# A linear-attention and gated FFN block on one NeuronCore: tokens as columns in the down and last attention products, two products summed in PSUM, another count of transfers, another order

## The chip, the core and the metric

The kernel runs on one core of a Trainium2 chip. The core has TensorE (PE) for matrix products, VectorE (DVE), ScalarE (ACT) and GpSimd (POOL) for elementwise work, and SyncE (SP), which issues the transfers between DRAM and the on-chip memory (SBUF). Products land in PSUM, which has 8 banks of 128 x 512 fp32. The metric is the device time of one execution in microseconds (us), as the median over runs.

## What is computed

x has 2048 tokens of width D = 512. A layer norm feeds two branches: linear attention with 32 heads of width 16, and a gated FFN of width F = 1792. The output is x plus the product of the two.

```python
phi = lambda t: jnp.where(t > 0, t + 1, jnp.exp(t)) + 1e-6
q, k, v = heads(xn @ wqkv)                      # xn = layernorm(x)
pq, pk = phi(q), phi(k)
kv = jnp.einsum("bhsd,bhse->bhde", pk, v)
z = jnp.einsum("bhsd->bhd", pk)
num = jnp.einsum("bhqd,bhde->bhqe", pq, kv)
den = jnp.einsum("bhqd,bhd->bhq", pq, z)[..., None] + 1e-6
s = (num / den) @ wo
g = silu((gelu(xn @ w_gate) * (xn @ w_up)) @ w_down)
return x + s * g
```

## The kernel before

**Precision.** Every large product is made in the fp32r format from operands split in two parts, hi and lo. `split` (L469) makes hi by a cast on ACT and lo = source − hi on DVE. `three` (L500) pairs them as hi·hi, hi·lo and lo·hi, so each product takes three matmuls per block of 128 in the summed dimension, and `Sum` (L475) issues them as separate steps into one PSUM bank.

**Strassen.** The large products use the seven-product Strassen-Winograd form, with the operand forms of `PRODUCTS` (L63). The seven products are summed into four results named 11, 12, 21 and 22; result 11 is product 1 plus product 2.

**First stage** (`first_products` L759, `rest` L787). Tokens are taken in eight pairs of 128-row tiles. Layer norm, transposes on PE, operand forms on POOL and splits give the matrices Xh and Xl. Pairs 0 and 1 make k and q plainly; pairs 2 to 7 make them by seven products, keys ("A", n, i). In `first_products` ACT saves product 1 (`e1`), PE makes product 2 in bank Y, and DVE adds the two. `gacc` (L747) sums the matrix from which kv follows, keys ("G", t, c), and POOL sums phi(k) into `zacc`. The X matrices of the first four pairs are written to DRAM (`spill_x`, L754) and read back for the second pass.

**FFN** (`ffn` L1127), in two passes over 1024 tokens: p = 1 has the second half of the tokens, p = 0 the first. Each pass has 7 units u of 256 gate and 256 up columns. A `quad` (L1037) makes the gate (even q) or the up part (odd q) of a unit by seven products ("F", q, i) of six 512-column matmuls: banks X = 0 or 1, Y = 2, Z = 3 or 4. Product 1 is saved by ACT (`fe`), product 2 goes to bank Y, and DVE adds. For the gate, ACT then takes gelu; for the up part, POOL multiplies by the gate. Result 21 has no add: ACT or DVE reads it from PSUM. Units 0 to 4 are multiplied with w_down by seven products ("E", p, u, v, i) in `down_strassen` (L1000), where h is the stationary operand and the down weights, 256 columns wide, are the moving one. Each bank of 512 columns takes two such regions r. DVE adds each bank to the sums `acc` (in the first unit ACT copies), whose tiles are 128 tokens by 512 features. Units 5 and 6 are multiplied plainly in `down` (L1095), keys ("D", p, u, j, c). The last of the eight tiles is made in two halves (`halves`, L1091).

**Attention** (`attn` L1229), between the passes. The matrix M (kv times wo) is made and split. `attn` then takes the 16 token tiles one by one, in the `order` 8, 0, 9, 1 and so on: a load of q, a product with z on POOL, the denominator and its reciprocal on DVE, the normalised tile pn, four transposes ("QT", i), a split, and twelve matmuls ("S", i) with pq stationary and M moving. Tiles 8 to 15 are multiplied by the finished g, x is added, and the result is stored; tiles 0 to 7 are stored as `s_d` and read back in `finish0` (L1288). z itself (`run_z`, L1196) is a product of ones with `zacc`, made amid the plain down products of pass 1, with the result in `zb`.

**Order.** Nothing runs in the order of the text. Each `do` (L121) records an operation with its engine and an estimated cost. `Plan.order` (L160) then simulates the engines (`forward`, L289) and picks, on each engine, the ready operation with the earliest due time. PE follows the list `pe_keys`, with a view of 6 us ahead (`AHEAD`). The draws of `KEPT` (L19) repeat fixed random changes of due times (`altered`, L183). The order that comes out is fixed in the program; on the chip each engine works through its own list and waits by semaphores. Transfers go through one list on SP; `forward` counts them by their size in KB and the constants `RATES` and `HELD`.

## Time and profile before

| | |
|---|---|
| median of 3 runs | 618.93 us (618.93 to 620.43) |
| profiled execution, its own time | 620.97 us |
| its span, first to last instruction | 619.3 us |
| granted TensorE clock, mean | 0.999 |
| DRAM traffic | 67.63 MB read, 44.56 MB written, 181 GB/s over the span |

The stages, as busy us of each engine in each stretch:

| stretch | us | PE | DVE | ACT | POOL |
|---|---|---|---|---|---|
| first stage, 8.68 to 136 | 127.32 | 125.07 | 107.36 | 96.03 | 64.96 |
| gate and up with down, pass 1, 136 to 328.7 | 192.70 | 192.65 | 163.24 | 107.67 | 92.85 |
| plain down and M, 328.7 to 357.3 | 28.60 | 28.60 | 22.83 | 11.50 | 10.70 |
| attention, 357.3 to 407.85 | 50.55 | 50.55 | 41.42 | 13.01 | 13.69 |
| pass 0, 407.85 to 613 | 205.15 | 205.15 | 139.25 | 89.48 | 47.23 |

In a row of groups, `L494 PE MATMUL FX<-Xh,w 128*128 128x512` names line, engine, operation, the tile written and those read, and the shape; after it come the count, the busy time and the mean ns of one. Line 494 is that of `Sum`'s matmul, so products are told apart by their tiles: FX, FY, FZ are gate and up, dX, dY, dZ the seven down products, d the plain ones, X, Y, Z the first stage, sps the attention's last product. A matmul's duration reaches from its start to its modelled end and overlaps the next; PEld is the load of the stationary operand. A row of waits has the engine, its line and tile, whom it waited for, and then the total in us, the number and the longest.

### The profile page before, as it was taken

The numbers are of one execution on the slowest core, as the hardware profiler recorded it, in microseconds if no ns is written. First come the engines' busy times: TensorE is split into PE (matmuls) and PEld (weight loads), VectorE is DVE, ScalarE is ACT, GpSimd is POOL, SyncE is SP. The second block draws the span as 40 slices with busy tenths as digits, with TensorE's granted clock in tenths as the row PEclk, the third lists the DMA queues.
The fourth block names the chain that finished last, engine by engine and source line by source line (L and its number), as shares of the span: only waits on it lengthen the run. The fifth ranks groups of instructions, "written<-read, shape, count | busy, mean of one in ns | idle before, by whom it ended". The sixth has DMA issues, their size and how long they took to land.

```text
span 619.3 us, 8717 instructions
## 1 busy us (share of the span) xinstructions
PE 611.5 (99%) x3156; PEld 517.6 (84%) x3156; DVE 481.3 (78%) x785; ACT 323.1 (52%) x582; POOL 233.8 (38%) x223
## 2 busy tenths in 40 slices
PE   9998999999999999999999999999999999999997
PEld 8886788878888888898888788888888888988886
DVE  6998797687788998999957799634567778786656
ACT  6676777685676464556444323244554334343433
POOL 4446743366635456452414344023031314111110
PEclk9999999999999999999999999999999999999999
DMA  7158740157726264435579755864433334343255
GB/s 263 61 160 269 227 144 36 54 199 263 300 69 271 73 268 154 186 135 206 225 246 399 303 171 186 321 222 177 178 131 145 139 133 153 120 152 120 69 166 191
DMA packets 49083, 112.77 MB, mean 182 GB/s; under 512 B 3088, under 2 KB 24848, under 8 KB 45456
## 3 DMA queue, kind: packets, MB, share of 16 engines
q1 hardware_dynamic: 49040, 112.21, 50.6%
q8 instruction: 25, 0.41, 0.3%
q14 instruction: 18, 0.15, 0.1%
HBM read 67.63 MB, written 44.56 MB: 181 GB/s over the span
## 4 chain that ended last, share of the span: by engine, by line
PE 95%; DVE 2%; DMA 2%; ACT 1%; issue 1%; SPq 0%; DVEq 0%; ACTq 0%
PE FX L494 25%; PE FZ L494 12%; PE dX L494 9%; PE sps L494 7%; PE d L494 7%; PE gps L494 6%; PE FY L494 6%; PE dZ L494 5%; PE X L494 5%; PE dY L494 2%; PE Z L494 2%; PE k L494 2%; PE q L494 2%; DMA x<-in_A_x 2%; PE Y L494 1%; PE ptq L1248 1%
## 5 line engine op out<-in xcount | busy, mean ns | idle before, releaser
L1062 POOL TENSOR_TENSOR h<-h,g 128x512 f32<-128x512 f32 x42 | 60.6, 1442 | 208.1 <-DVE h L467 199.9
L494 PE MATMUL FX<-Xh,w 128*128 128x512 f32 x448 | 134.6, 393 | 0.0
L494 PEld LDWEIGHTS FX<-Xh,w 128*128 128x128 f32 x448 | 80.0, 188 | 15.0 <-ACT fu L461 1.2
L494 PE MATMUL FX<-Xl,w 128*128 128x512 f32 x224 | 69.1, 393 | 0.0
L494 PE MATMUL FZ<-Xh,w 128*128 128x512 f32 x224 | 68.2, 391 | 0.0
L461 ACT COPY fu<-FX 128x512 f32<-128x512 f32 x56 | 32.7, 584 | 50.3 <-PE FX L494 48.6
L1021 DVE TENSOR_TENSOR acc<-acc,dX 128x512 f32<-128x512 f32 x64 | 43.7, 682 | 14.5 <-PE dX L494 13.7
L494 PEld LDWEIGHTS FZ<-Xh,w 128*128 128x128 f32 x224 | 40.5, 188 | 7.2
L494 PEld LDWEIGHTS FX<-Xl,w 128*128 128x128 f32 x224 | 40.0, 188 | 7.7 <-ACT fu L461 1.0
L467 POOL TENSOR_TENSOR u<-q,mstuff 128x512 f32<-128x512 f32 x16 | 22.8, 1438 | 33.2 <-DMA q<-q_d 24.5
L981 ACT ACTIVATE g<-g 128x512 f32<-128x512 f32 x42 | 26.6, 633 | 16.6 <-DVE g L467 14.2
L467 DVE TENSOR_TENSOR h<-fu,FZ 128x512 f32<-128x512 f32 x28 | 19.2, 684 | 20.4 <-ACT fu L461 17.3
L737 POOL TENSOR_TENSOR zacc<-zacc,kp 128x512 f32<-128x512 f32 x16 | 22.7, 1416 | 32.6 <-DVE kp L726 31.7
L461 ACT CAST hfh<-sums 128x512 fp32r<-128x512 f32 x40 | 24.4, 622 | 20.1 <-DVE sums L467 20.0
L494 PE MATMUL FY<-Xh,w 128*128 128x512 f32 x112 | 34.7, 393 | 0.0
L494 PE MATMUL FZ<-Xl,w 128*128 128x512 f32 x112 | 34.7, 391 | 0.0
L467 POOL TENSOR_TENSOR tmp<-raw 128x256 f32<-128x256 f32 x28 | 26.7, 967 | 20.9 <-DVE w L467 11.8
L1021 DVE TENSOR_TENSOR acc<-acc,dZ 128x512 f32<-128x512 f32 x40 | 27.3, 682 | 8.1 <-PE dZ L494 7.4
L494 PE MATMUL dX<-dh,hfl 128*128 128x256 f32 x160 | 32.2, 283 | 0.0
L494 PE MATMUL dX<-dl,hfh 128*128 128x256 f32 x160 | 32.2, 282 | 0.0
L467 DVE TENSOR_TENSOR g<-fu,FZ 128x512 f32<-128x512 f32 x28 | 19.1, 683 | 16.4 <-PE FZ L494 9.1
L494 PE MATMUL dX<-dh,hfh 128*128 128x256 f32 x160 | 31.9, 281 | 0.0
(196 smaller groups left out, 1580.2 us busy)
## 6 DMA issues: line engine op xcount, KB each, us to landing
w_d<-w SPq DMA_DIRECT2D x14, 1792.0 KB, 9.2
w<-w_d SPq DMA_DIRECT2D x14, 1792.0 KB, 7.3
draw<-in_B_w_down SPq DMA_DIRECT2D x14, 512.0 KB, 3.7
x<-in_A_x SPq DMA_DIRECT2D x16, 256.0 KB, 4.6
q_d<-qp SPq DMA_DIRECT2D x16, 256.0 KB, 2.0
q<-q_d SPq DMA_DIRECT2D x16, 256.0 KB, 3.3
xh_d<-Xh SPq DMA_DIRECT2D x4, 896.0 KB, 4.9
xl_d<-Xl SPq DMA_DIRECT2D x4, 896.0 KB, 6.3
```

What stands on the lines that cost most here:

```text
L461: do("ACT", act(n), lambda o, i: nc.scalar.copy(o, i), dst, src, name=name)
L467: do(eng, c, lambda o, p, q: getattr(e, f"tensor_{op}")(o, p, q), dst, a, b, name=name)
L494: nc.tensor.matmul(o if r is None else o[:, r], a, b, start=first, stop=made == self.passes[r], skip_group_check=self.on or r is not None)
L737: do("POOL", pool(D), lambda o, i: nc.gpsimd.tensor_add(o, o, i), zacc, p0, name="zacc")
L981: do("ACT", act(NC), lambda o, i: nc.scalar.activation(o, i, AF.Gelu_apprx_tanh), v, src, name="gelu")
L1021: do("DVE", dve(D), lambda o, i: nc.vector.tensor_add(o, o, i), o, ps, name="acc")
L1062: do("POOL", pool(NC), lambda o, i: nc.gpsimd.tensor_mul(o, o, i), h, g, name="h")
L1248: nc.tensor.transpose(o[:, k, :], a[:, k * P:(k + 1) * P], b)
```

## The change

It has five parts.

1. The seven down products take the down weights as the stationary operand and h, 512 tokens wide, as the moving one. The plain down products and the last product of the attention swap their operands in the same way. `acc`, `s_d` and the output hold features in rows and tokens in columns; the host passes x a second time, transposed, and transposes the output. `attn` works on four chunks of 512 tokens, each of which transposes four normalised tiles and makes four ("S", i, n).
2. In the first stage, in gate and up, and in the down products, ACT copies product 1 from its bank into bank Y (`seed`), and PE sums product 2 on top. The add of the two falls away; gelu or the product with the gate reads Y.
3. z is made amid quad 0 of pass 1, after its products 1, 2, 6, 5 and 7; its result goes back into `zacc`, and `zb` falls away.
4. The planner counts transfers otherwise: other KB for strided or spilled ones, other constants, and a hold of SP behind writes named `spill`. ACT's estimate tells PSUM from SBUF.
5. Other orders in `pe_keys` and a shorter `KEPT`; three plain down keys of unit 5 move into the last quad of pass 0.

```diff
 EPS = 1e-6
 KEPT = [
-    (-1, 12, [5000002, 5000009, 5000018, 5000019, 5000024, 5000044, 5000060]),
...
-        5000002, 5000007, 5000009, 5000014, 5000018, 5000022, 5000026, 5000031, 5000033, 5000034,
...
+    (-1, 12, [9100221, 9100222]),
+    (55, 70, [9100172]),
 ]
...
-RATES = 260.0, 380.0
-
-HELD = 1.9
+RATES = 260.0, 385.0
+HELD = 1.3, 2.6
+BEHIND = 2.8
 
...
-                dma = max(dma, o.end) + o.kb * (1.4 if o.kb == 896 else 1.0) / (RATES[0] if o.end < 3.0 else RATES[1])
-                o.lat = max(dma - o.end, o.kb / self.RATE) + (1.1 if o.end < 8.0 else HELD)
+                if written > o.end:
+                    o.end = free["SP"] = max(o.end, dma - BEHIND)
+                dma = max(dma, o.end) + o.kb / (RATES[0] if o.end < 3.0 else RATES[1])
+                if o.name == "spill":
+                    written = dma
+                o.lat = dma - o.end + HELD[o.end > 10.0]
...
-def act(n):
-    return 0.065 + 0.00084 * n
+def act(n, psum=False):
+    return 0.06 + (0.00083 if psum else 0.00095) * n
...
-    s_d = dram_view([S // 2, D], "s_d", NT // 2)
+    s_d = dram_view([D, S // 2], "s_d", NT // 2)
...
     def spill_x(n):
         for hl in "hl":
             dma(x_d[hl](n, (slice(None), slice(None), slice(n * P, (n + 1) * P))),
-                xrows(hl, 0, 7, [n]).map(lambda ap: ap.bitcast(F32)), 896)
+                xrows(hl, 0, 7, [n]).map(lambda ap: ap.bitcast(F32)), 1390, "spill")
 
     def first_products(n):
         ta = tokens[n][0]
         X = bank(0, f"X{n}")
         prod(X, n, 1, True)
-        e1 = saved(X, f"e1_{n}")
         split_xn(ta)
         Y = bank(2, f"Y{n}")
-        prod(Y, n, 2, True)
-        k_out(added(e1, Y, f"c11_{n}"), ta)
+        copy("ACT", Y, X, D, "seed")
+        prod(Y, n, 2, False)
+        k_out(Y, ta)
         return X
 
...
         pe_keys.append(("A", n, 4))
         g_take(2)
         pe_keys.append(("A", n, 3))
-        g_take(2)
         if more:
             pe_keys.append(("A", n + 1, 1))
+        g_take(2)
...
+    ones_r = const("ones_r", [P, P], F32R)
+    copy("ACT", ones_r, ones, P)
+    zh, zl = tile_in("up", 34, [P, D], F32R, "zh"), tile_in("up", 35, [P, D], F32R, "zl")
+    split(zh, zl, zacc, D, "z")
+    pz = bank(7, "pz")
+
...
+    copy("ACT", zacc, pz, D, "zb")
+    zb3 = zacc.map(lambda ap: ap.rearrange("p (h d) -> p h d", d=DH))
+    do("DVE", 0.59, lambda o, i: nc.vector.tensor_reduce(o, i, axis=AX.X, op=ALU.add), den_eps, zb3, port=False)
...
-        dma(raw, ext((up_k if i else gate_k)[:, :, u * 2 * P:(u + 1) * 2 * P]), 512)
+        dma(raw, ext((up_k if i else gate_k)[:, :, u * 2 * P:(u + 1) * 2 * P]), 900)
...
-            dma(w.map(lambda ap: ap.rearrange("p a s c -> p (a s c)").bitcast(F32)), w_d(q - NQ, q - NQ), 1792)
+            dma(w.map(lambda ap: ap.rearrange("p a s c -> p (a s c)").bitcast(F32)), w_d(q - NQ, q - NQ), 2220)
...
-        dma(w_d(q, q), w.map(lambda ap: ap.rearrange("p a s c -> p (a s c)").bitcast(F32)), 1792)
+        dma(w_d(q, q), w.map(lambda ap: ap.rearrange("p a s c -> p (a s c)").bitcast(F32)), 2220, "spill")
...
-        dma(raw, ext(down_f[:, 2 * u:2 * u + 2, :]), 512)
+        dma(raw, ext(down_f[:, 2 * u:2 * u + 2, :]), 620)
...
     def down_strassen(p, u, first):
 
-        for v in range(2):
-            X, Y, Z = (bank(5 + i, f"d{c}{p}{u}_{v}", (P, 2, 2 * P)) for i, c in enumerate("XYZ"))
+        for r in range(2):
+            X, Y, Z = (bank(i, f"d{c}{p}{u}_{r}") for i, c in zip((7, 6, 5) if r else (5, 6, 7), "XYZ"))
 
             def prod(ps, i, on):
                 a, b = PRODUCTS[i]
-                ws_, xs_ = three([[f[:, (2 * v + r) * P:(2 * v + r + 1) * P] for f in hforms[u, b]] for r in range(2)],
-                                 [ds[u, a]] * 2), None
-                Sum(ps, on).add(("E", p, u, v, i), *[[(*ab, r) for r, ab in enumerate(part)] for part in ws_],
-                                name="down", cost=SHORT)
+                Sum(ps, on).add(("E", p, u, r, i), *three([[f[:, r * P:(r + 1) * P] for f in ds[u, a]]], [hforms[u, b]]), name="down")
 
             def out(ps, key, new=False):
 
                 half, chunk = {11: (0, 0), 21: (1, 0), 12: (0, 1), 22: (1, 1)}[key]
-                pair = accp[p, 2 * chunk + v]
-                o = pair.part([pair.res[2 * r + half] for r in range(2)],
-                              (slice(None), slice(None), slice(half * 2 * P, (half + 1) * 2 * P)))
+                o = acc[p, 4 * chunk + 2 * half + r]
                 if first and new:
                     copy("ACT", o, ps, D, "acc")
                 else:
                     do("DVE", dve(D), lambda o, i: nc.vector.tensor_add(o, o, i), o, ps, name="acc")
             prod(X, 1, False)
-            out(X, 11, True)
-            prod(Y, 2, False)
-            out(Y, 11)
+            copy("ACT", Y, X, D, "seed")
+            prod(Y, 2, True)
+            out(Y, 11, True)
             prod(X, 6, True)
             out(X, 12, True)
             prod(Z, 5, False)
+            out(Z, 22, True)
             prod(X, 7, True)
-            out(X, 22, True)
-            out(Z, 22)
+            out(X, 22)
+            prod(Z, 3, True)
+            out(Z, 12)
             prod(X, 4, True)
             out(X, 21, True)
-            prod(Z, 3, True)
-            out(Z, 12)
...
     def quad(q, p):
         u, is_up = divmod(q % NQ, 2)
...
         X, Y, Z = bank(q % 2, f"FX{q}"), bank(2, f"FY{q}"), bank(3 + q % 2, f"FZ{q}")
         fprod(X, q, 1, True)
-        e1 = esaved(X, f"fe1_{q}")
-        fprod(Y, q, 2, True)
-        c_out(11, e1, Y)
+        copy("ACT", Y, X, NC, "seed")
+        fprod(Y, q, 2, False)
+        c_out(11, None, Y)
...
                 for u in units_:
-                    hh, hl = hs[p, u, key[0]], hs[p, u, key[1]]
-                    dh, dl = dws[p, u]
-                    total.add(("D", p, u, j, c), *three([(h[0][:, sl], h[1][:, sl]) for h in (hh, hl)],
-                                                       [(dh[i][:, cs], dl[i][:, cs]) for i in range(2)]),
+                    total.add(("D", p, u, j, c), *three([[f[i][:, sl] for f in dws[p, u]] for i in range(2)],
+                                                       [[f[:, cs] for f in hs[p, u, k]] for k in key]),
                               name="down", cost=PASS if m == 1 else SHORT)
...
+        early = [("D", p, SD[p], j, 0) for j in range(0 if p else 3)]
         for q in range(base, base + NQ):
...
-            for n, pair in enumerate(((q, 6), (q, 5), (q, 7), (q + 1, 1), (q + 1, 2), (q, 4), (q, 3))):
+            for n, pair in enumerate(((q, 6), (q, 5), (q, 7), (q + 1, 1), (q, 4), (q + 1, 2), (q, 3))):
                 if pair[0] < base + NQ:
                     keys.append(("F", *pair))
                 if i == 0 and n == 3 and 0 < u <= SD[p]:
-                    wait += [("E", p, u - 1, v, m) for v in range(2) for m in (1, 2, 6, 5, 7, 4, 3)]
+                    wait += [("E", p, u - 1, r, m) for r in range(2) for m in (1, 6, 5, 2, 7, 3, 4)]
                 for _ in range(min(2 if i else 1, len(wait))):
                     keys.append(wait.pop(0))
+                if early and q == base + NQ - 1 and pair[1] in (7, 4, 3):
+                    keys.append(early.pop(0))
         keys += wait
-        return keys, lambda j: [("D", p, u, j, c) for c in range(halves(p, j)) for u in plain_units]
+        return keys, lambda j: [key for c in range(halves(p, j)) for u in plain_units
+                                for key in [("D", p, u, j, c)] if key not in keys]
...
     pe_keys += keys1[:2]
     g_take(100)
-    pe_keys += keys1[2:]
+    pe_keys += keys1[2:5] + ["z"] + keys1[5:]
...
-    zh, zl = U("fx", FX, "zh", F32R), U("fx", FX, "zl", F32R)
-    split(zh, zl, zacc, D, "z")
-    pz = bank(2, "pz")
...
-    order = [t for a, b in zip(range(8, 16), range(8)) for t in (a, b)]
+    CHUNKS = [2, 0, 3, 1]
...
     def attn(i):
+        c = CHUNKS[i]
+        pns = []
+        for t in range(4 * c, 4 * c + 4):
...
+        forms_ = []
+        for k in range(KT):
+            pt = bank(ring("spt", [0, 1]), f"ptq{c}{k}", (P, 4, P))
+
+            def run_t(o, b, *a, k=k):
+                for j in range(4):
+                    nc.tensor.transpose(o[:, j, :], a[j][:, k * P:(k + 1) * P], b)
+            do("PE", 0.45, run_t, pt, ident, *pns, key=("QT", i, k))
+            ptf = pt.map(lambda ap: ap.rearrange("p j c -> p (j c)"))
+            f = [tile_in("up", places[i % 2][k][hl], [P, NC], F32R, f"pqT{hl}{c}{k}") for hl in range(2)]
+            split(*f, ptf, NC, "pqT")
+            forms_.append(f)
+        for n in range(KT):
+            ps = bank(ring("sps", [3, 4, 2]), f"sps{c}{n}")
+            Sum(ps).add(("S", i, n), *three([[M[hl].part(M[hl].res[k:k + 1], (slice(None), k, slice(n * P, (n + 1) * P))) for hl in range(2)]
+                                             for k in range(KT)], forms_), name="S")
+            at = slice(n * P, (n + 1) * P), slice(c * NC, (c + 1) * NC)
+            if c >= 2:
+                g = acc[1, 4 * (c - 2) + n]
+                xr = U("sxr", FACC, f"sxr{c}{n}")
+                dma(xr, ext(xT[at]), 256)
+                do("DVE", dve(D), lambda o, i: nc.vector.tensor_mul(o, o, i), g, ps)
+                tt("DVE", "add", g, g, xr, D)
+                dma(ext(outT[at]), g, 256)
+            else:
+                so = U("sxr", FACC, f"so{c}{n}")
+                copy("ACT", so, ps, D, "so")
+                dma(s_d(4 * c + n, at), so, 256)
+
+    held = [hs[1, u, key][hl].unit for key in (11, 21, 12, 22) for u in range(SD[1], NU) for hl in range(2)]
+    spots = [s for s in [*FHH, *FHL] if s not in held] + held
+    places = [[spots[2 * k:2 * k + 2] for k in range(b, b + KT)] for b in (0, KT)]
+    for i in range(4):
         attn(i)
-    pe_keys += last1(0) + last1(1) + ["z"] + last1(2) + last1(3) + last1(4)
+    pe_keys += last1(0) + last1(1) + last1(2) + last1(3) + last1(4)
     pe_keys += [("kv", g) for g in range(KT)] + last1(5) + [("m", g) for g in range(KT)]
-    pe_keys += last1(6) + [("QT", 0)] + last1(7)
-    for i in range(NT):
-        if i + 1 < NT:
-            pe_keys.append(("QT", i + 1))
+    pe_keys += last1(6) + [("QT", 0, 0), ("QT", 0, 1)] + last1(7) + [("QT", 0, 2), ("QT", 0, 3)]
+    for i in range(4):
+        for n in range(KT):
+            pe_keys.append(("S", i, n))
+            if i < 3 and n < 3:
+                pe_keys += [("QT", i + 1, n)] + [("QT", i + 1, 3)] * (n == 2)
...
-        n = halves(p, j)
-        sr = U("fs", [*FG, *FX], f"fs{j}", parts=n)
...
-        dma(sr, s_d(j, slice(j * P, (j + 1) * P)), 256)
-        dma(xr, ext(x[j * P:(j + 1) * P, :]), 256)
+        rows, c = slice((j % 4) * P, (j % 4 + 1) * P), j // 4
+        at = rows, slice(c * NC, (c + 1) * NC)
+        dma(sr, s_d(j, at), 256)
+        dma(xr, ext(xT[at]), 256)
+        w = NC // m
...
+    laid = {name: _np.ascontiguousarray(inputs[name]) for name in _INS}
+    laid["A_x"] = laid["A_x"].reshape(shape[-2], shape[-1])
+    laid["A_xT"] = _np.ascontiguousarray(laid["A_x"].T)
...
+    return _np.ascontiguousarray(r.results[0]["out_yT"].T).reshape(shape)
```

151 lines of the change are left out of this document (56 added, 95 removed), and 7 rows, old and new, of the table KEPT.

## The prediction

> **What bounds the kernel now.** I began with the page, its shares and its 40 slices.
>
> ```profile
> span 619.3 us, 8717 instructions
> ...
> PE 611.5 (99%) x3156; PEld 517.6 (84%) x3156; DVE 481.3 (78%) x785; ACT 323.1 (52%) x582; POOL 233.8 (38%) x223
> ...
> PE   9998999999999999999999999999999999999997
> PEld 8886788878888888898888788888888888988886
> DVE  6998797687788998999957799634567778786656
> ```
>
> PE is busy in every slice except the one near 54 us and the two ends; the next engine, DVE, has 78%. The profiled execution took 620.97 us for a span of 619.3, so 1.7 us lie around the span; the three runs have the median 618.93, 2.04 below this execution. I make the sum against 620.97 and take 2.04 off.
>
> Next I asked what PE waited for between the first real product (8.6 us) and the last (613 us).
>
> ```profile
> PE X L494 <- DVE qp L726: 2.0, 1, 2.0
> PE Z L494 <- DVE c L467: 0.3, 1, 0.3
> ```
>
> That is the whole list: 2.3 us. So the time is the sum of the matmuls in PE's order, a head and a tail. An edit counts if it makes PE's stream shorter, takes away these 2.3 us, or puts a wait into the stream. Relief for DVE, ACT and POOL counts only through waits.
>
> A matmul's own duration (393 ns for 512 columns) overlaps its successor's; what counts is the pitch. I took it from the chain of waits, in a stretch that has only 512-column matmuls:
>
> ```profile
> 422.99 2.72 PE FX L494 x12
> 425.71 1.36 PE FY L494 x6
> ```
>
> 2.72/12 = 0.2267 us each. Then I read the two stretches that hold the down products of each pass, from the first to the last 256-column matmul, and the groups by shape for their number:
>
> ```profile
> 169.53:309.80 140.27, 140.27 (x813) 123.31 (x812) 128.65 (x204) 77.97 (x144) 66.90 (x62) 1.00 0.46 176
> 435.07:575.49 140.42, 140.42 (x813) 123.15 (x812) 104.64 (x162) 59.21 (x106) 31.60 (x26) 1.00 0.38 139
> ```
>
> ```profile
> L494 PE MATMUL dX<-dh,hfl 128*128 128x256 f32 x160 | 32.2, 283 | 0.0
> ...
> L494 PE MATMUL dZ<-dh,hfl 128*128 128x256 f32 x80 | 16.0, 281 | 0.0
> ...
> L494 PE MATMUL dY<-dh,hfl 128*128 128x256 f32 x40 | 8.0, 281 | 0.0
> ```
>
> The window's columns are length, PE, PEld, DVE, ACT and POOL busy with counts, clock, DMA share and GB/s. Each of the three kinds (hi·hi, hi·lo, lo·hi) has 160 + 80 + 40 = 280 matmuls of 256 columns, so there are 840, or 420 in each stretch. One of the 813 began before its window, which leaves 392 of 512 columns. At 0.2267 those take 88.9 us, and the other 51.4 us fall on 420 narrow ones: 0.1225 each. PE is full in both stretches, and in the first DVE is at 92%.
>
> **Down products with tokens as columns.** For each of 7 products, 2 halves, 10 units and 3 kinds, two 256-column matmuls become one of 512: 840 go, 420 come. At 0.2267 the two stretches become 2 × 812 less 420, that is 1204 × 0.2267 = 272.9 us against 280.7: 7.8 us less. That is one end. For the other I looked at narrow matmuls in a row:
>
> ```profile
> 300.23 0.40 PE L494 MATMUL dX<-dl,hfh 128*128 128x256 f32 x2
> 300.46 0.40 PE L494 MATMUL dX<-dh,hfl 128*128 128x256 f32 x2
> 300.70 0.63 PE L494 MATMUL FX<-Xl,w 128*128 128x512 f32 x2
> ```
>
> Four of them start within 300.23 to 300.70, 0.47 us, or 0.235 a pair: only 0.008 above one wide matmul, times 420 = 3.5 us. The rest of the 7.8 sits in the 512-column matmuls of the stretch, of which six in a row take more than 1.36:
>
> ```profile
> 287.74 1.39 PE FY L494 x6
> 289.84 1.39 PE FX L494 x6
> ```
>
> Whether these return to 1.36 depends on whether mixing widths slows them. In the pure stretch around 425 us not one six is slow, so I take 7.2, near the upper end, and keep 3.5 to 7.8.
>
> The Trainium skill (TensorE: Matmul & The Clock Gate, Back-to-back issue gap) says a warm matmul follows the last after its columns divided by 2.4 plus 2.5 ns, which makes 215.8 ns for 512 columns and 109.2 for 256. By that rule a pair is only 2.5 ns dearer than one, and this edit would save an estimated 1.1 us. By that rule the trace disagrees: it has 226.7 ns and 117 to 122 ns.
>
> The stationary side changes from h to the down weights, with half as many loads (PEld has 88% of the stretch, beside PE): nothing. The plain down products and the attention's last product keep their number and width: nothing.
>
> **Two products summed in PSUM.** In 54 places (6 in the first stage, 28 in gate and up, 20 in down) product 2 now starts on a copy of product 1 that ACT writes into its bank.
>
> ```profile
> L461 ACT COPY fe<-FX 128x512 f32<-128x512 f32 x28 | 16.4, 585 | 6.5 <-PE FX L494 6.4
> ...
> L461 ACT COPY e<-X 128x512 f32<-128x512 f32 x6 | 3.5, 585 | 3.4 <-PE X L494 3.4
> ...
> L461 ACT COPY d<-acc 128x512 f32<-128x512 f32 x1 | 0.6, 591 | 0.7 <-DVE acc L1118 0.7
> ```
>
> ```profile
> L1021 DVE TENSOR_TENSOR acc<-acc,dY 128x512 f32<-128x512 f32 x20 | 13.6, 678 | 2.4 <-PE dY L494 2.2 <-issue 0.2
> ...
> L467 DVE TENSOR_TENSOR g<-fe,FY 128x512 f32<-128x512 f32 x14 | 9.5, 682 | 7.0 <-PE FY L494 6.3 <-ACT fe L461 0.6
> ...
> L467 DVE TENSOR_TENSOR h<-fe,FY 128x512 f32<-128x512 f32 x14 | 9.5, 679 | 2.7 <-PE FY L494 2.7
> ...
> L467 DVE TENSOR_TENSOR c<-e,Y 128x512 f32<-128x512 f32 x6 | 4.1, 679 | 0.6 <-PE Y L494 0.6
> ```
>
> ```profile
> L1062 POOL TENSOR_TENSOR h<-h,g 128x512 f32<-128x512 f32 x42 | 60.6, 1442 | 208.1 <-DVE h L467 199.9 <-ACT fu L461 6.1 <-ACT hh L461 2.0
> ```
>
> 34 ACT copies only change their target. No copy from PSUM to PSUM is in the trace; the copy out of PSUM takes 585 ns and the one into it 591, so I take 0.59 and would allow 0.5 to 0.7. ACT gains 20 × 0.59 = 11.8 us. DVE loses 20 + 14 + 6 adds, 13.6 + 9.5 + 4.1 = 27.2 us; where product 11 of the up half was added (14 times) DVE now multiplies by the gate, and POOL loses 14 × 1.44 = 20.2 us. On PE's account all of it is zero, because PE is at 100% beside it.
>
> New is the wait: product 2 needs product 1, the copy, and then PE again. Its length, from rows:
>
> ```profile
> 415.12 1.08 PE L494 MATMUL FX<-Xh,w 128*128 128x512 f32 x4
> ...
> 416.29 0.59 ACT L461 COPY fe<-FX 128x512 f32<-128x512 f32 x1
> ```
>
> ```profile
> 57.47 0.65 DVE L726 SCALAR_TENSOR_TENSOR qp<-X,qr 128x512 f32<-128x512 f32 x1
> 58.18 1.19 PE L494 MATMUL X<-kq,Xh 128*128 128x512 f32 x4 [1.97 <-DVE qp L726]
> ```
>
> The product ends at 416.20 and ACT starts 0.09 later. A PE that waits for DVE starts about 0.06 after it; I use that for ACT. Chain: 0.09 + 0.59 + 0.06 = 0.74, plus 0.17 by which a matmul's end (0.393) lags its pitch: 0.91 us of PE if nothing stood between. The new order puts one product of six (1.36) between, product 4 of the quad before, and in units 1 to 5 two to four down products more; in the first stage two G keys of three matmuls, 1.36 again; in the down products 6 and 5 stand between 1 and 2, and 6, which must not touch X before the copy has read it, has a gate or up product ahead of it. So the cover is 0.45 us where it is thinnest, in units 0 and 6. There ACT may be in the middle of another operation (0.6), and late by at most 0.2. What queues behind such a wait on PE is the rest of its order; behind the copy on ACT, the next h and g conversions. Range 0 to 54 × 0.91 = 49; I take +0.2.
>
> **Attention in four chunks of 512 tokens.** PE's work is unchanged: 64 transposes and 192 matmuls.
>
> ```profile
> 357.53 2.76 PE sps L494 x12
> 360.73 2.77 PE sps L494 x12
> ```
>
> ```profile
> L461 ACT CAST pqTh<-ptq 128x512 fp32r<-128x512 f32 x16 | 9.4, 587 | 15.0 <-PE ptq L1248 15.0
> ```
>
> ```profile
> L467 DVE TENSOR_TENSOR pqTl<-ptq,pqTh 128x512 fp32r<-128x512 f32 x16 | 10.8, 678 | 4.1 <-ACT pqTh L461 4.1
> ```
>
> ```profile
> 357.30:407.85 50.55, 50.55 (x252) 41.76 (x250) 41.42 (x78) 13.01 (x24) 13.69 (x9) 1.00 0.61 210
> ```
>
> One S key with its four transposes takes 3.20 us, as it will. What changes is the grouping: the first transpose of a chunk needs all four normalised tiles, and its first S key all four splits. DVE is 82% busy here and keeps the same number of operations, so over 12.8 us (four keys) it has 2.3 to spare. The last split of the next chunk takes about 0.6 + 0.7 plus hops, 1.5 us, behind the S key placed after it (2.76): covered. The first chunk has only its own beginning: transposes 2 and 3 stand directly before S, at most two casts and a sub, 2 × 0.59 + 0.68 = 1.9 us, if PE's order takes nothing else in between. Bounds 0 to 1.9, and 7.6 if every chunk does it; I take +0.4. The loads of x and the stores of s and y keep their number and size (256 KB in rows of 2 KB) and pass SP's queue in another order; nothing on PE waits for them but the buffers of S.
>
> **z moved forward.** The two pz matmuls go from the plain down products to the first quad, with two casts, a sub, a copy and a reduce.
>
> ```profile
> L737 POOL TENSOR_TENSOR zacc<-zacc,kp x16: 1287/1298/1839, 15.1 to 139.0; 128x512 f32<-128x512 f32 x16
> ```
>
> POOL's last sum starts at 139.0 and ends near 141; the z key stands behind 8 G keys (24 matmuls, 5.4 us of PE) and three products (4.1) that begin about there, and its cast and sub take 1.3. It moves past no DMA. Zero; up to 1 us if POOL ends later.
>
> **Count of transfers and new order.** This changes no instruction, only their order. What it can reach is the wait of 2.3 us, whose cause the chain of waits shows:
>
> ```profile
> 45.96 5.41 DMA x<-in_A_x
> ```
>
> An x tile was asked for late and came 5.41 us later, DVE stood in its queue, and PE behind DVE. An order that counts spilled writes higher and holds SP back behind them may ask earlier. Bounds: 2.3 gained, or as much lost by a new wait of the kind; I take half, 1.1 gained. Plain down keys drawn into the last quad leave no gap to fill: zero.
>
> **Sum.** −7.2 + 0.2 + 0.4 + 0 − 1.1 = −7.7: 613.3 for a profiled execution, 611.2 for the median.
>
> **The rivals.**
>
> *The pitch of the wide matmuls stays slow* (1.39 per six), because something else in the stretch slows them: the down edit gives 3.5, the sum −4.0, 614.9. For it: the narrow ones in a row are at 0.235 a pair. Against: no slow six in the pure stretch.
>
> *A narrow matmul has no price of its own*: two take the 0.2267 of one wide, and all that the stretch takes beyond that comes from waits and weight loads that stay. Then the down edit gives 0, the sum is −0.5, and the time 618.4: no change. Against it stand the 0.235 a pair, with PE waiting for nothing. The Trainium skill's gap (same section) comes near this case.
>
> *Attention gives it back.* Every chunk's first S key waits for its splits: 7.6 in place of 0.4, the sum −0.5, 618.4: no change. For it: DVE at 82% and whole groups of four. Against: one S key of cover at each border.
>
> *The copies stall PE: slower.* Place: product 2 of the 28 quads and 20 down halves and the 6 of the first stage. If ACT reaches each copy 0.8 us late because its queue holds conversions that wait for DVE or POOL, each stalls 0.8 − 0.45 = 0.35 us; 54 of them are 19 us, time 630. It turns slower than before where the mean stall passes 7.7/54 = 0.14 us. For it: ACT's queue is in order and of the 28 copies that it replaces only 8 waited for PE, so the others ran when ACT came to them. Against: there they had slack, DVE is relieved by 27 us, and units 1 to 5 have far more cover.
>
> *The order does better:* all of the 2.3 goes, no new wait comes, and the down edit reaches 7.8: −10.1, 608.8.
>
> **How the numbers follow.** Forecast 60%, order better 10%, pitch slow 13%, no price 4%, attention 6%, copies stall 7%. What a measurement tells from no change is about 0.3%, 1.9 us, so faster means under 617.07. Forecast, better order and slow pitch lie there, as does some of the attention case for a partial loss: faster 0.86. Same: the case of no price and the rest of attention, 0.06. Slower: copies and a little of the others, 0.08. The range takes the better order with 1.8 us to spare for the runs' own spread (618.93 to 620.43 is 1.5) and the slow pitch on the other side: 607.0 to 615.5.
>
> **What would show it.** PE should have 2736 matmuls in place of 3156, the d groups X, Y, Z 512 columns wide with 420 in all, and the stretch of down products in each pass about 136.5 us long with sixes of 1.36. DVE near 454 us, ACT near 335, POOL near 214. PE's waits should stay under 3 us together, with no copy into PSUM on the list. A list of PE waits for ACT copies, or of S keys for pqT, would prove the forecast wrong; so would sixes that remain at 1.39.

## The result and the profile after

| | before | after |
|---|---|---|
| median, runs side by side on one chip | 619.68 us (618.93 to 620.70, 4 runs) | 613.00 us (612.22 to 613.14, 4 runs) |
| ratio, 95% interval | | 0.9889 (0.9868 to 0.9909) |
| profiled execution, its own time | 620.97 us | 613.08 us |

The change made the kernel 1.1% faster. The medians lie 6.7 us apart, and 613.00 is 1.8 above the forecast of 611.2. The profiled execution lost 7.9 us where the sum had 7.7. In the page of the changed kernel, the shares and two of the engines' slices:

```profile
span 611.3 us, 7799 instructions
...
PE 604.2 (99%) x2736; PEld 497.0 (81%) x2736; DVE 464.9 (76%) x745; ACT 334.2 (55%) x602; POOL 211.7 (35%) x209
...
PE   9999999999999999999999999999999999999997
...
DVE  6999888677799999999757698714566868686456
```

The slice near 54 us that PE did not fill before is full now. The counts are those forecast: 2736 matmuls, and 40 operations fewer on DVE (785 to 745). ACT and POOL are near the 335 and 214 forecast; DVE has 465 us where 454 were expected, because operations that stayed became longer on balance. One group shows it, hfl from sums (40 operations), in the kernel before and then in the changed one:

```profile
L467 DVE TENSOR_TENSOR hfl<-sums,hfh 128x512 fp32r<-128x512 f32 x40 | 27.4, 700 | 0.0
```

```profile
L459 DVE TENSOR_TENSOR hfl<-sums,hfh 128x512 fp32r<-128x512 f32 x40 | 31.0, 786 | 0.2
```

The mean of one went from 700 to 786 ns, 3.6 of the 11 us; the splits of w, Xl and dl became longer too, while hfl from h became shorter (805 to 735 ns). What makes the difference was not tested. A count times an old mean is only a first guess for DVE. All that PE waited for from 8.6 to 606 us:

```profile
PE ptq L1241 <- DVE pn L1231: 1.1, 2, 0.7
PE FX L486 <- ACT fu L453: 0.2, 1, 0.2
PE dX L486 <- ACT dY L453: 0.2, 1, 0.2
```

The 2.3 us for qp and c are gone; 1.1 us in the attention and 0.4 us behind ACT copies are new. The second row is the old kind of copy (`fu`, a sum saved from PSUM to SBUF), and only the third is a copy into PSUM: one late copy on the list, of 54. Next, the windows from the first to the last matmul of the seven down products in each pass (length, PE, PEld, DVE, ACT, POOL busy with counts, clock, DMA share, GB/s):

```profile
167.64:302.59 134.95, 134.95 (x595) 111.38 (x594) 128.05 (x190) 81.54 (x153) 61.30 (x62) 1.00 0.51 197
430.21:565.90 135.69, 135.23 (x596) 111.36 (x595) 95.36 (x148) 64.11 (x114) 23.52 (x21) 1.00 0.38 140
```

Each has 594 matmuls (one or two more began ahead of it), and 594 × 0.2267 = 134.7. The forecast had 602 and 136.5: the new order leaves 8 fewer gate and up matmuls in each. In the chain of waits between 168 and 186 us the sixes read:

```profile
170.76 1.39 PE FY L486 x6
...
172.84 1.36 PE FZ L486 x6
...
174.88 1.36 PE FX L486 x6
...
177.60 1.36 PE FZ L486 x6
```

At 1.36 three of the four are at the pitch of the stretch that had no narrow ones; the first, at 1.39, comes right behind matmuls that started late. The three kinds of copy into PSUM, as groups by shape:

```profile
L453 ACT COPY FY<-FX 128x512 f32<-128x512 f32 x28 | 16.2, 579 | 4.2 <-PE FX L486 4.1
...
L453 ACT COPY dY<-dX 128x512 f32<-128x512 f32 x20 | 11.3, 566 | 21.0 <-DVE acc L1024 14.0 <-PE dX L486 6.8
...
L453 ACT COPY Y<-X 128x512 f32<-128x512 f32 x6 | 3.4, 570 | 5.0 <-PE X L486 5.0
```

They cost 566 to 579 ns, where 590 was taken. One thing was not foreseen. The loads of q, by their row in the list of transfers, take 7.6 us from issue to landing in the median, against 3.3 before:

```profile
q<-q_d SPq DMA_DIRECT2D x16, 256.0 KB, 7.6
```

SP's queue shows a part of why:

```profile
344.69 0.32 SPq L449 DMA_DIRECT2D q<-q_d  x1
348.47 3.65 SPq L449 DMA_DIRECT2D Xh<-xh_d  x7
...
356.59 3.75 SPq L449 DMA_DIRECT2D q<-q_d  x4
```

Seven loads of 512 KB bring Xh back for pass 0, and they now go out at 348.47, ahead of seven q loads; the four at 356.59 took 6.2 to 7.7 us each. In the kernel before, q loads issued between 357 and 384 us took 2.5 to 4.1. (Loads of q that go out earlier, beside those for M, are slow in both kernels: up to 10.7 us before and 10.9 after.) Before, the copy of z (`zb`) lay in the place of Xh until the last u had read it, so the reload went out at 387.38, behind all of q. Part 3 of the change removed that lock without saying so.

### The profile page after: what moved, and what is told of

The parts are those of the page before. It is cut to its first block, busy times and chain, and to the rows that moved or that the text cites. A ratio compares the mean times of both kernels' runs of the same rounds, so it can differ in the third digit from the quotient of the medians.

```text
span 611.3 us, 7799 instructions
## 1 busy us (share of the span) xinstructions
PE 604.2 (99%) x2736; PEld 497.0 (81%) x2736; DVE 464.9 (76%) x745; ACT 334.2 (55%) x602; POOL 211.7 (35%) x209
## 4 chain that ended last, share of the span: by engine, by line
PE 92%; DVE 5%; DMA 1%; issue 1%; ACT 0%; POOL 0%; SPq 0%; ACTq 0%; POOLq 0%
PE FX L486 24%; PE FZ L486 12%; PE dX L486 9%; PE gps L486 7%; PE d L486 7%; PE FY L486 6%; PE X L486 6%; PE dZ L486 4%; PE Z L486 3%; PE sps L486 3%; PE dY L486 2%; PE k L486 2%; PE q L486 2%; PE Y L486 1%; PE pt L651 1%; PE warm L516 1%
## 5 line engine op out<-in xcount | busy, mean ns | idle before, releaser
L1065 POOL TENSOR_TENSOR h<-h,g 128x512 f32<-128x512 f32 x28 | 38.6, 1377 | 185.2 <-DVE h L459 185.2
L486 PEld LDWEIGHTS FX<-Xh,w 128*128 128x128 f32 x448 | 83.8, 188 | 18.5 <-ACT fu L453 1.3
L1024 DVE TENSOR_TENSOR acc<-acc,dX 128x512 f32<-128x512 f32 x52 | 35.4, 680 | 15.9 <-PE dX L486 15.9
L459 POOL TENSOR_TENSOR sums<-draw 128x256 f32<-128x256 f32 x20 | 19.8, 1002 | 51.1 <-DMA draw<-in_B_w_down 27.4
L459 POOL TENSOR_TENSOR u<-q,zacc 128x512 f32<-128x512 f32 x16 | 20.8, 1318 | 44.3 <-DMA q<-q_d 31.6
L486 PE MATMUL sps<-pqT,M_hi 128*128 128x512 f32 x128 | 32.3, 393 | 0.0
L453 ACT CAST hfh<-h 128x512 fp32r<-128x512 f32 x30 | 18.5, 622 | 24.1 <-DVE h L459 16.3
L486 PE MATMUL dX<-hfh,dh 128*128 128x512 f32 x80 | 31.2, 390 | 0.2 <-ACT dY L453 0.2
L486 PE MATMUL dX<-hfl,dh 128*128 128x512 f32 x80 | 31.2, 390 | 0.0
L459 DVE TENSOR_TENSOR hfl<-sums,hfh 128x512 fp32r<-128x512 f32 x40 | 31.0, 786 | 0.2
```

The lines of the kernel that those rows point to most:

```text
L453: do("ACT", act(n, src.psum), lambda o, i: nc.scalar.copy(o, i), dst, src, name=name)
L459: do(eng, c, lambda o, p, q: getattr(e, f"tensor_{op}")(o, p, q), dst, a, b, name=name)
L486: nc.tensor.matmul(o if r is None else o[:, r], a, b, start=first, stop=made == self.passes[r], skip_group_check=self.on or r is not None)
L1024: do("DVE", dve(D), lambda o, i: nc.vector.tensor_add(o, o, i), o, ps, name="acc")
L1065: do("POOL", pool(NC), lambda o, i: nc.gpsimd.tensor_mul(o, o, i), h, g, name="h")
```

## Experiments

The kernels of one group of runs shared the chip and the runs of the kernel before, whose median was 620.24 us for the first four kernels below, 621.18 for old_count, the strict ones and saved_no_draws, 621.52 for the two with the reload put late, and 620.53 for the last two. Across groups the ratios are compared. "No draws" means that the list `KEPT` is empty, so that two kernels differ by a part of the change and not also by draws that were fitted to one of them.

**Width alone.** Every engine has the order of the changed kernel, instruction by instruction, but each down matmul is issued as two of 256 columns.

```diff
+    whole = nc.tensor.matmul
+    def in_halves(o, a, b, start, stop, **more):
...
+        whole(o[:, 0:256], a, b[:, 0:256], start=start, stop=stop, **more)
+        whole(o[:, 256:512], a, b[:, 256:512], start=False, stop=stop, **more)
...
+        nc.tensor.matmul = in_halves if o.key and o.key[0] == "E" else whole
         o.fn()
```

> The changed kernel with the same order of work on every engine; only each of the 420 matmuls of the seven down products is issued as two of 256 columns with the same stationary operand, so this part is as narrow as before. Theory (width: 0.1225 us for a narrow matmul in company, and the wide ones around it slowed to 1.39 per six): 7.2 to 8 us slower than the changed kernel, about 620.5. Rival 1 (only the narrow ones' own 0.235 a pair counts, sixes stay at 1.36): 3.5 us slower, 616.5. Rival 2 (narrow ones have no price, the gain came from the order): 613.

> The changed kernel again, as the measure of the other runs: 613.0 within 0.6.

| | median us | ratio to before (620.24) |
|---|---|---|
| narrow_down | 619.77 (619.42 to 620.97) | 0.9990 (0.9976 to 1.0004) |
| after_again | 612.07 (611.88 to 612.52) | 0.9855 (0.9829 to 0.9882) |

Width alone is worth 619.77 − 612.07 = 7.7 us, at the upper end of the 3.5 to 7.8. The same two windows of narrow_down, and rows of its chain of waits after 435 us:

```profile
167.43:306.45 139.02, 138.94 (x806) 122.36 (x805) 127.49 (x190) 81.89 (x154) 61.57 (x62) 1.00 0.49 191
433.03:572.33 139.30, 138.86 (x806) 122.28 (x805) 97.87 (x148) 64.24 (x115) 25.19 (x21) 1.00 0.36 137
```

```profile
435.53 0.12 PE dX L1312
435.65 0.12 PE dX L1313
435.77 0.12 PE dX L1312
436.01 1.39 PE FY L486 x6
438.11 1.39 PE FZ L486 x6
```

The stretches are 139.02 + 139.30 − 134.95 − 135.69 = 7.7 us longer (those of after_again are within 0.02 us of the two of the changed kernel), so all of the difference lies in them. The slow sixes of 1.39 are back, with the same order on every engine; the lists of waits differ outside of these stretches alone, by 0.9 us more in the first stage and 0.6 less in the attention. From start to start of all matmuls in the stretches, the 420 pairs take 101.2 us against 96.0 for 420 wide ones (241 ns a pair against 229), and the 768 gate and up matmuls between them 177.1 against 174.7 (230.6 ns against 227.4). So both ways of loss are real: 5.2 us in the narrow ones themselves, 2.4 in their neighbours. Both rivals on the down edit fall.

Two limits remain. Each half also loads its stationary operand again (PEld has 805 loads in the first stretch, against 594), so the run does not tell the price of the width from that of the loads. And the narrow matmuls of the kernel before were a little cheaper: by the same measure 237 ns a pair, with the wide ones at 230.9. Between the two kernels the stretches gained 280.69 − 270.64 − 16 × 0.2267 = 6.4 us, where the last term stands for the 16 wide matmuls that went elsewhere.

The Trainium skill (TensorE: Matmul & The Clock Gate, Back-to-back issue gap) gives the gap of an isolated warm matmul as its columns over 2.4 plus 2.5 ns, and says itself that this under-counts where the columns are few. By that formula the 420 matmuls more would have cost an estimated 1.1 us. The trace disagrees: in this stream they cost 7.7. The prediction left out that the formula is meant for an isolated matmul.

**The rest of the change, without draws.**

```diff
-KEPT = [
...
-]
+KEPT = []
```

> The changed kernel without the draws of KEPT: the planner's own first order, everything else alike. If the draws are what keeps PE's waits at 1.5 us: 614.5 to 617, with waits of 1.5 us or more in the first stage. If the planner's first order is as good on the chip: 613 within 1.

> The kernel before without the draws of KEPT. If the draws are what keeps its PE waits at 2.3 us: 621 to 625. If not: 619.7 within 1. The difference to the changed kernel without draws is what the rest of the change gives under the planner's own order: the theory says 7 to 8 us, a rival that puts the gain in the newly chosen draws says 4 or less.

Changed kernel without draws: 614.94 us (614.52 to 615.56), ratio 0.9900 (0.9881 to 0.9919). Kernel before without draws: 620.44 (618.63 to 621.24), ratio 0.9986 (0.9971 to 1.0001). The new draws are worth 2.9 us to the changed kernel; the old ones brought the old kernel nothing measurable. Without draws the change is worth 620.44 − 614.94 = 5.5 us, between the two expectations. If the width is worth 7.7 there too, which no run tests, the rest loses 2.2 us, and the draws give that back. The time of after_no_draws came as expected, but not its sign: the first stage has 0.7 us of waits on its list, not 1.5. The gain of the draws lies mostly early: the first gate product starts 132.43 us into the span of after_again and 135.94 us into that of after_no_draws. Of these 3.5 us, 1.4 are six G matmuls that after_again makes later, and 1.0 lies ahead of the first transpose (where two executions of the changed kernel differ by 0.6). after_again itself came out at 612.07, below the expected 612.4 to 613.6.

**The count of transfers of before.**

```diff
-                if written > o.end:
-                    o.end = free["SP"] = max(o.end, dma - BEHIND)
-                dma = max(dma, o.end) + o.kb / (RATES[0] if o.end < 3.0 else RATES[1])
...
+                dma = max(dma, o.end) + o.kb * (1.4 if o.kb == 896 else 1.0) / (RATES[0] if o.end < 3.0 else RATES[1])
+                o.lat = max(dma - o.end, o.kb / self.RATE) + (1.1 if o.end < 8.0 else 1.9)
...
-                xrows(hl, 0, 7, [n]).map(lambda ap: ap.bitcast(F32)), 1390, "spill")
+                xrows(hl, 0, 7, [n]).map(lambda ap: ap.bitcast(F32)), 896)
```

> The changed kernel without draws, with the count of transfers of before (KB, rates, held times, no hold of SP). Theory (the stricter count takes away waits for late x tiles in the first stage): 1 to 2.5 us slower than the changed kernel without draws, with a PE wait or late x load in the first stage. Rival (the draws alone did it): within 0.7.

617.80 us (617.11 to 619.10), ratio 0.9947 (0.9927 to 0.9967): 2.9 us slower than after_no_draws, so the stricter count is worth something, but not where it was looked for. The first gate product starts within 0.2 us of that of after_no_draws, and no wait of the first stage is on its list that after_no_draws does not have. Of the 3.5 us between the two profiled executions, 3.1 have come up by the first S matmul, in the M stage. Its waits there and its chain of waits:

```profile
PE pm L1191 <- DVE mstuff L1184: 1.6, 1, 1.6
...
PE pkv L1181 <- DMA mstuff<-g_d: 0.4, 2, 0.2
```

```profile
334.20 10.91 DMA q<-q_d
...
345.24 1.30 POOL u L442
...
346.56 0.69 DVE den L1209
347.25 0.61 DVE mstuff L1184
...
347.90 1.13 PE pm L1191 x2
```

The order on DVE makes the wait. Here `den`, which needs u and with it a load of q, stands ahead of `mstuff`, the mask that the matmuls for M need, so M waits for q. In after_no_draws the mask comes first:

```profile
344.23 0.69 DVE L1188 TENSOR_TENSOR mstuff<-pkv,mask 128x512 f32<-128x512 f32 x1 [2.88 <-PE pkv L1185]
345.14 0.69 DVE L1213 TENSOR_REDUCE den<-u 128x32 f32<-128x512 f32 x1 [0.21 <-POOL u L446]
```

The transfers themselves do not explain it. This load of q took 10.9 us, the one in its place in after_no_draws 10.5, and the transfers are busy for 90% of the stage here against 96% there. A count that expects q too early would lead to such an order; that this is why the planner chose it was not tested.

**The order of the copies' cover.** PE takes its list strictly (no view ahead), once with the new key order and once with the old one, in which product 2 stands right behind the next product 1.

```diff
-    AHEAD = 6.0
+    AHEAD = 0.0
```

```diff
-((q, 6), (q, 5), (q, 7), (q + 1, 1), (q, 4), (q + 1, 2), (q, 3))
+((q, 6), (q, 5), (q, 7), (q + 1, 1), (q + 1, 2), (q, 4), (q, 3))
```

> The changed kernel without draws, and PE kept strictly to the written list (AHEAD 0 in place of 6 us). Both theories only use it as the base of the next run; the view ahead should be worth several us: 618 to 640.

> As the run before, but gate and up in the written order of before, where product 2 of the next quad stands right behind its product 1. In units 0 and 6 nothing then stands between them, six times in both passes. Theory (chain of 0.91 us of PE from the end of product 1 over the copy to product 2): PE waits of about 0.7 to 0.9 us each for the copies FY, 5 to 6 us slower than the strict run. Rival (the chain is shorter, or hidden in any case): within 1.5 us.

The new keys, strictly: 626.83 us (626.32 to 627.65), ratio 1.0092 (1.0068 to 1.0116). The old keys, strictly: 635.88 (634.18 to 637.49), ratio 1.0237 (1.0205 to 1.0269), 9.0 us more. The row of PE's waits for the copy, with the new keys and then with the old ones:

```profile
PE FY L473 <- ACT FY L440: 1.6, 2, 0.9
```

```profile
PE FY L473 <- ACT FY L440: 6.4, 10, 0.7
```

Of the ten exposed copies eight have nothing between: the six that were counted, and the first quad of each pass, where product 2 stands right behind product 1 under either order. These eight wait 0.69 us each; with the 0.17 by which a matmul's end lags its pitch that is 0.86, where the prediction's chain had 0.91. The other two have three down matmuls between and wait 0.43. With the new keys only the first quads are left (at 144.45 and 418.79 us), so no copy with a product between is on the list. The eight added waits, with their 0.17, are about 6 of the 9.0 us; I had expected 5 to 6 in all, and the rest was not taken apart.

**Product 1 saved and added again in gate and up** (28 places; no draws):

```diff
-        copy("ACT", Y, X, NC, "seed")
-        fprod(Y, q, 2, False)
-        c_out(11, None, Y)
+        e1 = esaved(X, f"fe1_{q}")
+        fprod(Y, q, 2, True)
+        c_out(11, e1, Y)
```

> The changed kernel without draws, and in gate and up product 1 is saved by ACT and added by DVE as before (28 places); first stage and down products keep the sum in PSUM. Compared with the changed kernel without draws (614.9). Theory (the sum in PSUM only relieves DVE and POOL beside a full PE and its waits are covered): within 1 us, with DVE up by 9.5 us and POOL by 20. Rival 1 (the waits for the copies cost PE): 2 us or more faster. Rival 2 (the relief of DVE and POOL is what makes the order work): 2 us or more slower.

625.15 us (624.04 to 626.98), ratio 1.0066 (1.0044 to 1.0088): about 10 us slower than after_no_draws. My expectation failed by far. First the windows of the attention, from its first S matmul to the first matmul of pass 0, of after_no_draws and then of this kernel; then its chain of waits, ahead of that window:

```profile
354.63:404.55 49.92, 49.83 (x244) 40.89 (x242) 37.29 (x70) 12.55 (x23) 10.18 (x9) 1.00 0.56 203
```

```profile
358.51:414.81 56.30, 52.03 (x243) 42.02 (x242) 41.11 (x73) 11.99 (x22) 12.88 (x10) 0.97 0.51 176
```

```profile
351.40 5.03 DMA Xh<-xh_d
...
356.51 8.61 DMA q<-q_d
...
365.25 1.30 POOL u L446
...
371.22 0.96 PE ptq L1228 x5
372.18 3.23 PE sps L473 x8
```

6.4 of the 10 us lie here. A load of q waits in SP's queue behind the reload of Xh (3.6 MB), takes 8.61 us itself, and POOL, DVE and PE stand behind it one after the other.

PE is idle for 56.30 − 52.03 = 4.3 us, against 0.1 in after_no_draws. The other 2.2 are longer matmuls: PE's longest wait (3.63 us) ends at 371.22, and for 3.41 us from 371.65 its granted clock is 0.50, so that eight sps matmuls take 3.23 us where eight at full pitch take 1.8. The mean granted clock was 0.993 to 0.997 in all six executions of this kernel, and 0.998 to 1.000 in those of after_no_draws. Two readings were open: the early reload, or the load on DVE and POOL.

**The reload later, first try.** The planner is told that the reload comes behind the loads of q; the program gets no new wait.

```diff
+            q_loads.append(plan.ops[-1])
...
+            if hl == "h":
+                for o in q_loads:
+                    if o not in plan.ops[-1].pre:
+                        plan.ops[-1].pre.add(o)
+                        o.suc.append(plan.ops[-1])
```

> The changed kernel without draws, with one thing more: the reload of Xh for the second pass (3.6 MB) stands on SP's list behind the last load of q, as it did before the change. Theory (with zb gone the reload moved ahead of the attention, and q loads behind it land late, which is what the attention's waits come from): the attention stage 0.3 to 0.8 us shorter, the time 0 to 1 below the changed kernel without draws. Rival (the waits come from DVE): no difference in that stage.

> The run with product 1 of gate and up saved and added (28 places), and also with the late reload. Theory (most of its 10 us came from q loads behind the reload): the attention's excess falls from 7.5 to 2 us or less and the time to 616 to 619; what then remains above the run before is the price of the 28 adds, 1 to 4 us. Rival (the load on DVE alone delays the normalised tiles): 623 or more.

late_reload_no_draws: 618.08 us (616.93 to 618.69), ratio 0.9949 (0.9929 to 0.9969), 3.1 us slower than without the edit, against what I had expected. saved_late_no_draws: 620.79 (619.86 to 625.01), ratio 1.0002 (0.9984 to 1.0019), about 4 us faster than saved_no_draws and between its two expectations. The edit did only half of what it was meant to do: in late_reload_no_draws three pieces of the reload went out at 353.76, still ahead of seven loads of q, and of the other four the last alone came behind them all. So these runs did not decide. They show one thing more: the planner makes a new order for every edit, and here an edit of the order alone cost 3.1 us.

**The reload later, by data.** `zb` is put back: ACT copies z into the last rows of Xh's place, as in the kernel before, and the reload cannot start until the last u has read it. One ACT copy more (0.6 us).

```diff
+    zb = mt.part(mt.res[6:7], (slice(None), 12))
+    copy("ACT", zb, zacc, D, "zb2")
+    zb3 = zb.map(lambda ap: ap.rearrange("p (h d) -> p h d", d=DH))
```

> The changed kernel without drawn places, with the sum of z copied into the last rows of x's place again (one more ACT copy of 0.6 us), as the kernel before has it: the reload of x's high part can then start only after the last u has used the copy, so behind the loads of q. If the time of the reload is what puts q late (theory), q lands in about 3 to 5 us in place of the 7 to 8 of the changed kernel, PE's waits in the attention fall from about 1.2 to 0.8 or less, and the time is 614 to 615.5, since without the saved products little was lost there. Rival (the grouping of four tiles makes the wait, whatever the loads do): the wait for pn stays at 1 us or more and the time is the same or 0.5 above.

> As zb_back_no_draws, and the 28 gate and up halves save product 1 and add it on DVE as before. Theory (of the 10 us that the saved products cost without draws, about 6 are a collision of the reload of x's high part with the loads of q, the rest is the price of the 28 additions on DVE and POOL in pass 1 and the last stage): the attention's waits fall from 7.5 us to 2 or less and the time is 617 to 620. Rival (the load on DVE and POOL alone delays the attention, the reload only happens to lie there): the attention's waits stay at 5 us or more and the time is 623 or more.

| no draws | reload as in the change | reload held by `zb` |
|---|---|---|
| copies into PSUM (as changed) | 614.94 (614.52 to 615.56), ratio 0.9900 (0.9881 to 0.9919) | 614.87 (614.32 to 615.69), ratio 0.9912 (0.9887 to 0.9938) |
| gate and up saved and added | 625.15 (624.04 to 626.98), ratio 1.0066 (1.0044 to 1.0088) | 620.57 (619.64 to 621.72), ratio 0.9998 (0.9980 to 1.0015) |

SP's queue in saved_zb_no_draws shows that the reload now goes out last, at 385 us, and the window of its attention is back near that of after_no_draws:

```profile
377.52 1.58 SPq L436 DMA_DIRECT2D q<-q_d  x2
385.07 0.32 SPq L436 DMA_DIRECT2D Xh<-xh_d  x1
385.92 3.34 SPq L436 DMA_DIRECT2D Xh<-xh_d  x6
```

```profile
359.83:410.96 51.13, 50.68 (x242) 41.42 (x241) 39.24 (x72) 12.11 (x22) 13.01 (x10) 0.98 0.63 215
```

So some 4 to 5 us of the 10 were the early reload (625.15 to 620.57; 0.7% by the two ratios), with the lower clock that came behind its wait; in the profiled executions the attention is 5.2 us shorter, 51.13 against 56.30. Its waits on the list fell from 5.7 to 2.3 us, a little above the 2 that I had expected and far from the rival's 5. I had expected 617 to 620, so the collision is a little smaller and the rest a little larger than I thought: with the reload held, the 28 saved products cost 620.57 − 614.87 = 5.7 us.

With the copies, the early reload costs nothing that can be measured: q takes 4.4 us in zb_back_no_draws by the list of transfers, 7.1 in after_no_draws, and the times are equal. The wait for pn is on neither's list, so these two do not tell what makes it in the changed kernel with its draws. Its trace does: the longer of the two waits (0.7 us, ended at 374.35) comes after DVE has been busy for all of the 8.30 us from 366.00 and for 13.50 of the 13.60 before that, so it is DVE's own work that is late there. Only the shorter one (0.35 us, ended at 384.90) has a q load in its chain, issued at 372.53 and landed 4.57 us later. Whether late q loads had pushed DVE's work together was not tested.

Part of the 5.7 us shows as waits of pass 1 in saved_zb_no_draws:

```profile
PE dX L473 <- DVE hfl L446: 1.8, 2, 1.0
PE dX L473 <- ACT dY L440: 0.7, 1, 0.7
```

DVE has 476.0 us there against 461.3 in zb_back_no_draws, and the splits of h come late. The attention has 2.3 us of waits that zb_back_no_draws does not have, and behind one of them (1.46 us) the profiled execution was again granted a clock of 0.50 for 3.41 us, an estimated 1.7 us lost (half of 3.41); ten of its twelve executions have a mean clock of 0.998 or more, too high for that. The rest of the 5.7 us was not taken apart, and how much of it is the load on DVE and POOL and how much the new order was not tested. No run was faster than the changed kernel.

## Why the prediction was right, step by step

*PE's stream sets the time.* It held: PE is at 99% in both kernels. Of the 7.9 us between the two profiled executions 6.4 lie in the two stretches of down products, and the width alone is 7.7 of the 8.2 us between after_again and the kernel before on the same chip (620.24).

*Down width, −7.2.* Measured 7.7 at the same order. The choice between 3.5 and 7.8 was right, for the reason given: the slow sixes were caused by the narrow matmuls beside them and go with them. The split was off: in narrow_down the narrow ones themselves cost more (5.2, a pair at 241 ns and not 235), the neighbours less (2.4). In the kernel before a pair took 237 ns, nearer to the 235. Between the two kernels themselves the stretches gained 6.4, not 7.2 to 7.8: the new stream has some 1.2 us of stalls in them, 1.0 of it near 460 us, where the change's chain runs through three sums on DVE and a late copy.

*Copies into PSUM, +0.2, with DVE and POOL relief at zero.* The copies and their cover held: 0.57 to 0.58 us each, and one wait of 0.2 us where none was to be on the list. That relief is worth nothing was the weak step. No run gives it to the kernel before by itself; in the changed kernel without draws, with the reload held, taking it back in 28 of 54 places costs 5.7 us. That the relief pays for slack that other parts of the change use up is a reading that is not shown. The forecast came out because both would be in it: by narrow_down, all of the change but the width is worth 619.77 − 620.24 = −0.5 us (ratio 0.9976 to 1.0004), and the other terms were 0.2 + 0.4 + 0 − 1.1 = −0.5. That these agree to the digit is luck: the interval is 1.7 us wide, and narrow_down's pairs are 1.5 us dearer in sum than those of the kernel before.

*Attention, +0.4.* Measured 1.1 in the profiled execution (0.8 in after_again): inside its bounds of 0 to 1.9, as a wait for pn and not for the casts and splits that I had counted. The step gave DVE 2.3 us to spare in every 12.8; the trace has it busy for 21.8 of the 21.9 us ahead of the longer wait.

*z, 0.* Its key stalls nothing, but the step was incomplete: I looked at the queues that z moves past and not at the place that it had occupied. Its going freed the reload of Xh. In the changed kernel without draws this costs nothing measurable; with the 28 products saved again it cost 4 to 5 us.

*Count and order, −1.1.* The 2.3 us of waits did go. The sum of the parts has another shape: without draws the rest of the change loses about 2.2 us (if the width is worth 7.7 there), the draws gain 2.9, and the new count, already in the run without draws, is worth 2.9, nearly all of it in the M stage and not in the first stage. The prediction looked at waits that the kernel before had, and so could not see one that the new order would have had with the old count. Half of 2.3 was a guess that fitted.

*From the profiled execution to the median, −2.04.* This step did not hold. The profiled execution of the changed kernel, 613.08, lies at its median, 613.00, where the one of the kernel before lay 2.04 above its own. So the sum was right for the profiled executions (613.3 forecast) and 1.8 us off for the median.

*The rivals.* Slow pitch and free narrow ones fall by narrow_down. The copies that stall PE need an order without cover: the strict runs show their price, and the changed kernel has one such wait on its list. The attention gave back 1 us, not 7. The better order is not what came: its 608.8 needs no new wait, and there are 1.5 us of new ones.

## What to carry to other kernels

Where TensorE is full, count its matmuls by pitch and look at the pitch of the neighbours too: 840 narrow matmuls turned into 420 wide ones saved 12 ns in each pair and 3 ns in each of the wide ones between. Work taken off an engine that nothing waits for need not be worthless in the new order: here giving a part of it back cost 5.7 us. Test it by giving the work back, not by the old waits alone, and remember that each such edit also makes a new order. When a buffer is given up, ask which transfer it had been holding back. Where an engine works through a fixed list, look at what stands ahead of the operation that the full engine needs: one `den` ahead of the mask made M wait for a load that M does not read.

## What was not expected of the hardware

A 512-column matmul amid 256-column ones keeps a pitch of 230.6 ns against 227.4 when all are 512 wide, at a granted clock of 1.00 and with the same order on every engine. A 256 KB load that went out 5.5 us after the first of seven 512 KB loads took 8.61 us to land (saved_no_draws); with the reload held, the load at the same place took 3.6 (saved_zb_no_draws). Right behind a wait of 3.63 us PE was granted half its clock for 3.41 us (saved_no_draws), and behind one of 1.46 us too (saved_zb_no_draws), but not behind one of 1.97 us in the kernel before. ACT copied 128 x 512 from PSUM to PSUM in 566 to 579 ns, no slower than from PSUM to SBUF (585).
